# A streaming decode block: GpSimd's half-sums taken out, pairs of heads evicted inside PSUM, one weight block split differently

## The chip, the cores and the metric

The kernel runs on one core of a Trainium2 chip. The metric is device microseconds from one execution, the median of three runs. Lower is better.

## The reference

One token goes through an adaptive-LayerNorm block with cached attention and a squared-ReLU feed-forward part. All data are float32, D = 640, 32 heads of 192, 8192 cached keys and values per head, feed-forward width 1536.

```python
mod = (silu(c) @ w_mod).reshape(1, 6, 1, 640)      # sa, ca, ga, sb, cb, gb
h = layernorm(x) * (1 + ca) + sa
q = (h @ wq) split into 32 heads of 192
p = softmax(q . k_cache * 192**-0.5)               # 32 x 8192
x = x + ga * ((p . v_cache) joined @ wo)
h = layernorm(x) * (1 + cb) + sb
x = x + gb * (relu(h @ w1 + b1)**2 @ w2 + b2)
```

The two caches are 201 MB each; every byte of them is read once.

## The kernel before, in words

The caches and the weights `wq` and `wo` are laid out on the host as 53 chunks, each one slice of at most 84 x 192 = 16128 floats in each of the 128 partitions. `plan()` (L55) writes down what each chunk holds: some key positions (`nk`, 64 positions per partition make a head), some units of values (`nv`, eight units make a head) and now and then a piece of `wq` or `wo`. Most chunks hold 44 key positions and 5 value units.

All loads go through SyncE's one queue, in program order, into three slots of SBUF that are used in turn. `load(n + 3)` (L240) may start when everything that reads chunk n is done, so the queue is at most three chunks ahead. The first slot of all holds `wm0`, the first two modulation blocks with the first piece of `wq` (L122), and behind it `wm0x`: part of the columns of the last of its five row blocks, 128 rows, which the table `XP` deals over some of 64 partitions in up to seven steps and which six small loads bring (L125). A small load has 8, 3 or 1 of these partitions.

For the keys of a chunk VectorE does nearly everything. `multiply` (L273) multiplies every key with the query in place. Then, for the last 7/16 of the chunk's positions, GpSimd adds the upper 96 of the 192 products to the lower 96 (L399, "folds" them), while VectorE sums the other 9/16 (`scores`, L281). VectorE then sums the folded positions over 96 elements. Scores stand in a ring `sc`. When a head's 64 positions are complete, `softmax` takes the maximum over partitions with a TensorE transpose and ScalarE writes the exponentials `p`. For an odd head, ScalarE spreads the two sums of a pair (`wide`), TensorE turns them over the partitions (L310), and `inverse` sums the result (L288) and takes its reciprocal.

For the values, TensorE multiplies `p` with each unit (L322) into one PSUM bank per head. The bank holds eight products side by side of which a mask picks one. `evict` (L334, L336) multiplies by the mask into SBUF and sums over the eight, for each head apart; after an odd head TensorE transposes the pair (L340) and VectorE sums over the copies (`turn`, L344). `attend` (L352 to L356) then multiplies with `wo` into `att_a`.

After the last chunk come the other modulation blocks (`mod(2, 3)`, `gate`), the second LayerNorm, `w1` (L447), the squared ReLU, and `w2` (L464), whose four pieces are the last loads of the queue.

Of the kernel before, what the change touches and what calls it, by code (L numbers as in the profile page):

```python
# [93 lines left out]
def block_kernel(ctx: ExitStack, tc: tile.TileContext, kv, wm0, wm0x, wm1, w1, w2, out):  # L94
# [89 lines left out]
    def mod(first, n, w, wx=None, between=lambda: None):  # L184

        ps = psum.tile([P, 512], F32, tag="q", name=f"ps_mod{first}", bufs=2)
        for b in range(KB):
            if b == 3:
                between()
            wb = w[:, b * n * D:(b + 1) * n * D]  # L190
            if wx is None or b < KB - 1:
                wb = wb.rearrange("p (m n) -> p m n", m=n)
                parts = [(g, slice(0, n * DG), wb[:, :, DG * g:DG * (g + 1)]) for g in range(G)]
            else:
                wb = wb[:, :n * 3 * DG].rearrange("p (m n) -> p m n", m=n)
                parts = [(g, slice(0, n * DG), wb[:, :, DG * g:DG * (g + 1)]) for g in range(2)] + [(2, slice(0, DG), wb[:, 0, 2 * DG:])]
            for g, at, wg in parts:
                nc.tensor.matmul(ps[32 * g:32 * (g + 1), at], e[:, b:b + 1].to_broadcast([P, 32]), wg,  # L198
                                 start=(b == 0), stop=(b == KB - 1 and (wx is None or g < 2)))
# [86 lines left out]
    def inverse(i):  # L286
        r = work.tile([P, 1], F32, tag="r", name=f"r{i}")
        nc.vector.tensor_reduce(r, sum_t.pop(i), axis=AX.X, op=ALU.add)  # L288
        nc.vector.reciprocal(r, r)
        ri_t[i] = r  # L290

    def softmax(h):
# [34 lines left out]
    def evict(h):  # L327

        n = 32 * NV
        if h % 2 == 0:  # L330
            os_t["part"] = work.tile([P, 2, ED], F32, tag="os", name=f"os{h // 2}")
        os_ = os_t["part"]
        om = work.tile([P, ED, E], F32, tag="om", name=f"om{h}", bufs=1)
        nc.vector.tensor_mul(om[:n], ps_t.pop(h)[:n].rearrange("p (d e) -> p d e", e=E),  # L334
                             mask[:n, None, :].to_broadcast([n, ED, E]))
        nc.vector.tensor_reduce(os_[:n, h % 2], om[:n], axis=AX.X, op=ALU.add)  # L336
        if h % 2:
            i = h // 2
            os_t[i] = psum.tile([P, 512], F32, tag="sm", name=f"ps_oT{i}", bufs=2)
            nc.tensor.transpose(os_t[i][:, :n], os_[:n].rearrange("p a d -> p (a d)"), ident[:n, :n])  # L340

    def turn(i):
        oT = work.tile([P, NV], F32, tag="oT", name=f"oT{i}")
        nc.vector.tensor_reduce(oT, os_t[i][:, :96].rearrange("p (j r) -> p j r", j=NV), axis=AX.X, op=ALU.add)  # L344
        os_t[i] = oT
# [177 lines left out]
```

## Time and profile before

| | |
|---|---|
| median of three runs | 1051.96 us (1051.89 to 1052.2) |
| the profiled execution, its own time | 1051.94 us |
| its span, from the first to the last instruction | 1050.0 us |
| VectorE busy | 826.1 us (79%) |
| TensorE busy | 488.7 us (47%) |
| GpSimd busy | 190.4 us (18%) |
| DMA | 452.14 MB, mean 431 GB/s |

The execution's own time is 1.94 us longer than its span. The profile names an instruction by its line in the kernel, its engine, and output <- input by the program's names. DVE is VectorE, PE TensorE (PEld its weight loads), ACT ScalarE, POOL GpSimd and SP SyncE. "Idle" is the time an engine stood still ahead of an instruction, and behind the arrow stands what ended it.

### The profile page before, as it was taken

What the parts mean: (1) busy time and instruction counts of PE and PEld (TensorE: products, weight loads), DVE (VectorE), ACT (ScalarE), POOL (GpSimd) and SP (SyncE); (2) the same over time, 40 slices, a digit from 0 to 9 for tenths busy, and PEclk for the clock granted to TensorE, in tenths of its full rate; (3) what the DMA queues carried; (4) which work ended last, traced back from release to release, by engine and by line L of the source; (5) the groups of instructions that cost most, each with busy time, mean ns of one, the idle gap of its engine ahead of it and who ended that gap; (6) DMA issues with size and microseconds to landing.
All of it is one profiled execution on the core that took longest, in us unless ns stands there. A gap on an engine that the chain in (4) does not pass through costs nothing.

```text
span 1050.0 us, 5180 instructions
## 1 busy us (share of the span) xinstructions
PE 488.7 (47%) x2130; PEld 133.8 (13%) x2130; DVE 826.1 (79%) x405; ACT 44.9 (4%) x122; POOL 190.4 (18%) x61
## 2 busy tenths in 40 slices
PE   3253334455352363446354356345445346435287
PEld 1010001111010010101011011001011011001023
DVE  1799878876959969888697895999887977988812
ACT  0100000000000000000000000000000000000001
POOL 1113121121212211212121121122211211311200
PEclk9676576777685686668776576686777767768689
DMA  9999999999999999999999999999999999999998
GB/s 408 430 433 432 434 435 433 446 439 433 431 432 433 428 433 433 433 442 434 432 434 433 433 434 437 435 433 435 436 430 433 433 435 433 435 433 426 431 429 345
DMA packets 9144, 452.14 MB, mean 431 GB/s; under 512 B 1033, under 2 KB 1037, under 8 KB 1421
## 3 DMA queue, kind: packets, MB, share of 16 engines
q1 hardware_dynamic: 9118, 451.83, 99.5%
q8 instruction: 16, 0.26, 0.1%
q14 instruction: 6, 0.05, 0.0%
q10 hardware_dynamic: 4, 0.00, 0.0%
HBM read 451.82 MB, written 0.00 MB: 430 GB/s over the span
## 4 chain that ended last, share of the span: by engine, by line
DMA 53%; DVE 33%; PE 12%; ACT 1%; issue 0%; SPq 0%; DVEq 0%; ACTq 0%
DMA chunk<-in_kv 50%; DVE chunk L273 17%; DVE sc L281 13%; PE ps_o L322 6%; PE ps_q L254 2%; PE att_a L354 2%; DMA w_t<-in_w 2%; DMA wm_t<-in_wm 1%; DVE os L336 1%; DVE om L334 1%; PE ps_mx L297 1%; PE att_a L356 1%; ACT p L305 0%; PE ps_mod L198 0%; PE ps_mod L204 0%
## 5 line engine op out<-in xcount | busy, mean ns | idle before, releaser
L273 DVE TENSOR_TENSOR chunk<-chunk,qb 128x8064 f32<-128x8064 f32 (+19 forms) x81 | 419.6, 5211 | 127.3 <-DMA chunk<-in_kv 122.1
L281 DVE TENSOR_REDUCE sc<-chunk 128x25 f32<-128x4800 f32 (+21 forms) x109 | 333.8, 3096 | 0.4
L399 POOL TENSOR_TENSOR chunk<-chunk 128x1824 f32<-128x1824 f32 (+9 forms) x51 | 187.3, 3673 | 801.0 <-DVE chunk L273 568.6
L322 PE MATMUL ps_o<-chunk,p 128*32 128x512 f32 x1536 | 288.6, 719 | 70.1 <-DMA chunk<-in_kv 60.6
L297 PE MATMUL ps_mx<-ident,mp 128*128 128x128 f32 x32 | 14.6, 457 | 347.6 <-DVE mp L295 347.5
L322 PEld LDWEIGHTS ps_o<-chunk,p 128*32 128x32 f32 x1536 | 66.2, 129 | 268.1 <-issue 183.2
L354 PE MATMUL att_a<-chunk,oW 128*32 128x512 f32 x96 | 66.5, 850 | 45.0 <-ACT oW L352 45.0
L254 PE MATMUL ps_q<-chunk,ln_h 128*128 128x512 f32 x110 | 64.5, 746 | 25.2 <-DMA chunk<-in_kv 25.2
L297 PEld LDWEIGHTS ps_mx<-ident,mp 128*128 128x128 f32 x32 | 5.7, 177 | 376.3 <-DVE mp L295 308.2
L305 ACT ACTIVATE p<-sc,nm 128x256 f32<-128x256 f32 x32 | 16.2, 507 | 651.0 <-DVE nm L299 651.0
L254 PEld LDWEIGHTS ps_q<-chunk,ln_h 128*128 128x128 f32 x110 | 25.9, 246 | 61.6 <-issue 33.1
L334 DVE TENSOR_TENSOR om<-ps_o,mask 96x512 f32<-96x512 f32 x32 | 21.6, 675 | 8.9 <-PE ps_o L322 8.9
L299 DVE TENSOR_REDUCE nm<-ps_mx 128x1 f32<-128x128 f32 x32 | 9.3, 292 | 19.6 <-PE ps_mx L297 19.6
L354 PEld LDWEIGHTS att_a<-chunk,oW 128*32 128x32 f32 x96 | 12.4, 145 | 82.4 <-ACT oW L352 47.6
L336 DVE TENSOR_REDUCE os<-om 96x64 f32<-96x512 f32 x32 | 21.8, 682 | 1.1
L344 DVE TENSOR_REDUCE oT<-ps_oT 128x3 f32<-128x96 f32 x16 | 4.0, 248 | 18.4 <-PE ps_oT L340 18.4
L310 PE MATMUL ps_sum<-ident,wide 128*128 128x128 f32 x16 | 7.5, 467 | 22.4 <-ACT wide L308 22.4
L340 PE MATMUL ps_oT<-ident,os 96*128 96x96 f32 x16 | 4.9, 306 | 26.9 <-DVE os L336 26.9
L198 PE MATMUL ps_mod<-wm_t,silu 128*32 128x480 f32 (+2 forms) x78 | 9.1, 606 | 14.4 <-DVE silu L180 14.4
L356 PE MATMUL att_a<-chunk,oW 128*96 128x384 f32 x32 | 14.5, 536 | 0.0
L352 ACT ACTIVATE oW<-oT,r 128x96 f32<-128x96 f32 x16 | 5.9, 372 | 173.3 <-DVE oT L344 173.3
L255 ACT ACTIVATE qb<-ps_q 128x512 f32<-128x512 f32 x12 | 7.2, 597 | 130.6 <-PE ps_q L254 130.6
(79 smaller groups left out, 99.8 us busy)
## 6 DMA issues: line engine op xcount, KB each, us to landing
chunk<-in_kv SPq DMA_DIRECT2D x38, 8064.0 KB, 35.3
chunk<-in_kv SPq DMA_DIRECT2D x11, 8000.0 KB, 36.6
chunk<-in_kv SPq DMA_DIRECT2D x2, 7872.0 KB
chunk<-in_kv SPq DMA_DIRECT2D x1, 6144.0 KB, 22.8
wm_t<-in_wm SPq DMA_DIRECT2D x1, 4480.0 KB
wm_t<-in_wm SPq DMA_DIRECT2D x1, 4257.0 KB, 12.5
chunk<-in_kv SPq DMA_DIRECT2D x1, 3264.0 KB
chunk<-in_kv SPq DMA_DIRECT2D x1, 3072.0 KB
```

The source lines that it names most:

```text
L254: nc.tensor.matmul(ps, h1[:, b:b + 1].to_broadcast([P, P]), w[:, b], start=(b == 0), stop=(b == KB - 1))
L273: nc.vector.tensor_mul(pr, pr, q[:, None, :].to_broadcast([P, b - a, DH]))
L281: nc.vector.tensor_reduce(sc[:, a % SRING:a % SRING + b - a], src[:, a - first:b - first], axis=AX.X, op=ALU.add)
L297: nc.tensor.transpose(ps[:, :P], mp.to_broadcast([P, P]), ident)
L299: nc.vector.tensor_reduce(nm, ps[:, :P], axis=AX.X, op=ALU.max, negate=True)
L305: nc.scalar.activation(p, s[:, :, None].to_broadcast([P, NPOS, 32 // E]), AF.Exp, bias=nm, accum_out=sp[:, h % 2:h % 2 + 1])
L322: nc.tensor.matmul(ps_t[h][32 * g:32 * (g + 1)], p[:, E * j:E * (j + 1)].rearrange("p e r -> p (e r)"), t[:, g], start=(j == 0), stop=last)
L334: nc.vector.tensor_mul(om[:n], ps_t.pop(h)[:n].rearrange("p (d e) -> p d e", e=E), mask[:n, None, :].to_broadcast([n, ED, E]))
L336: nc.vector.tensor_reduce(os_[:n, h % 2], om[:n], axis=AX.X, op=ALU.add)
L354: nc.tensor.matmul(att_a[96:, :512], oW[:, j], w[:, j, :512], start=(first and j == 0), stop=(last and j == NV - 1))
L356: nc.tensor.matmul(att_a[:96, :NV * (D - 512)], oW.rearrange("p j r -> p (j r)"), w[:, :, 512:], start=first, stop=last)
L399: nc.gpsimd.tensor_add(half, half, kt[:, m:, DH // 2:])
```

## The change

1. GpSimd no longer folds. `scores` gets the whole chunk, so VectorE sums all positions over 192 elements in one instruction. The ring `sc` is twice as long, so that it wraps half as often.
2. Pairs of heads share one PSUM tile of two banks (two such tiles in place of three single banks). `evict` multiplies by the mask in place in PSUM and sums, once for a pair (for the last pair, once for each head).
3. The sum over the copies (`turn`) goes to TensorE: the matmul at the end of `evict` has `part` (ones for each group of 32 rows) where the identity was, and its three columns are the result. The sum in `inverse` goes there as well, by a matmul with ones.
4. PSUM tag `q` has one bank in place of two. `ps_f` moves to the tag of the pairs.
5. The last block of `wm0` (640 columns for each of its two modulations) is split so that the small loads carry 4 x 160 columns of each row in place of 3 x 160, and `XP` deals them in other portions. `mod(0, 2)` reads them with 28 passes of 320 columns where it had 14 of 160 and 14 of 320.
6. Two copies at the start (`spread`) go from VectorE to ScalarE.

```diff
-POOL = 7
-SRING = 4 * NPOS
+SRING = 8 * NPOS
-XP = ((32, 8, 5), (0, 3, SX), (1, 3, SX), (2, 3, SX), (3, 3, 6), (33, 1, SX))
-WX = 3 * DG
+XP = ((32, 8, SX), (33, 8, 4), (0, 3, SX), (1, 3, 3), (2, 1, SX), (3, 1, 3))
+WX = 4 * DG
...
         if wx is not None:
...
-                for g, at, wg in ((2, slice(DG, 2 * DG), wx[:, s, :DG]), (3, slice(0, 2 * DG), wx[:, s, DG:])):
-                    nc.tensor.matmul(ps[32 * g:32 * (g + 1), at], e[:64, KB + s:KB + s + 1].to_broadcast([64, 32]), wg,
-                                     start=False, stop=(s == SX - 1))
+                for g in range(2, G):
+                    nc.tensor.matmul(ps[32 * g:32 * (g + 1), :n * DG], e[:64, KB + s:KB + s + 1].to_broadcast([64, 32]),
+                                     wx[:, s, g - 2], start=False, stop=(s == SX - 1))
...
     def gate(m, w, steps):
 
-        ps = psum.tile([P, 512], F32, tag="q", name=f"ps_mod{m}", bufs=2)
+        ps = psum.tile([P, 512], F32, tag="q", name=f"ps_mod{m}", bufs=1)
...
     def inverse(i):
         r = work.tile([P, 1], F32, tag="r", name=f"r{i}")
-        nc.vector.tensor_reduce(r, sum_t.pop(i), axis=AX.X, op=ALU.add)
-        nc.vector.reciprocal(r, r)
+        nc.vector.reciprocal(r, sum_t.pop(i))
...
-            nc.tensor.transpose(ps[:, :P], wide.rearrange("p a d -> p (a d)"), ident)
-            sum_t[h // 2] = ps[:, :P]
+            nc.tensor.matmul(ps[:, :1], wide.rearrange("p a d -> p (a d)"), ones[:, :1], start=True, stop=True)
+            sum_t[h // 2] = ps[:, :1]
...
-        if j == 0:
-            ps_t[h] = psum.tile([P, 512], F32, tag="o", name=f"ps_o{h}", bufs=3)
+        if j == 0 and h % 2 == 0:
+            ps_t[h // 2] = psum.tile([P, 2, 512], F32, tag="o", name=f"ps_o{h // 2}", bufs=2)
...
+    def evict(first, last):
+
+        n, i = 32 * NV, first // 2
+        a, b = first % 2, last % 2 + 1
+        po = ps_t[i][:n, a:b].rearrange("p a (d e) -> p a d e", e=E)
+        nc.vector.tensor_mul(po, po, mask[:n, None, None, :].to_broadcast([n, b - a, ED, E]))
+        if a == 0:
+            os_t[i] = work.tile([P, 2, ED], F32, tag="os", name=f"os{i}")
+        nc.vector.tensor_reduce(os_t[i][:n, a:b], po, axis=AX.X, op=ALU.add)
+        if b == 2:
+            nc.tensor.matmul(ps_t[i][:, 0, :NV], os_t.pop(i)[:n].rearrange("p a d -> p (a d)"), part[:n, :NV],
+                             start=True, stop=True)
...
         if nk:
             multiply(kt, kp, nk)
-            m = nk - POOL * nk // 16
-            half = kt[:, m:, :DH // 2]
-            nc.gpsimd.tensor_add(half, half, kt[:, m:, DH // 2:])
...
-        for h in evicted:
-            evict(h)
+        for heads in evicted:
+            evict(*heads)
         if nk:
-            scores(kt[:, :m], kp)
-        for h in evicted:
-            if h % 2:
-                turn(h // 2)
-        if nk:
-            scores(half, kp + m)
+            scores(kt, kp)
```

How the instructions stand on VectorE for the third and fourth chunk, before (44 key positions each; `ps_o` is a head's PSUM bank, `sc` the ring of scores):

```order
L273 TENSOR_TENSOR chunk_178<-chunk_178,qb 128x6528
L273 TENSOR_TENSOR chunk_178<-chunk_178,qb 128x1920
L281 TENSOR_REDUCE sc<-chunk_178 128x25
L281 TENSOR_REDUCE sc<-chunk_178 128x19
L295 TENSOR_REDUCE mp_238<-sc 128x1
L299 TENSOR_REDUCE nm_242<-ps_mx_240 128x1
L273 TENSOR_TENSOR chunk_193<-chunk_193,qb 128x8448
L288 TENSOR_REDUCE r_276<-ps_sum_248 128x1
L289 RECIPROCAL r_276<-r_276 128x1
L334 TENSOR_TENSOR om_280<-ps_o_202,mask 96x512
L336 TENSOR_REDUCE os_279<-om_280 96x64
L281 TENSOR_REDUCE sc<-chunk_193 128x25
```

The same place in the changed kernel:

```order
L280 TENSOR_TENSOR chunk_179<-chunk_179,qb 128x6528
L280 TENSOR_TENSOR chunk_179<-chunk_179,qb 128x1920
L288 TENSOR_REDUCE sc<-chunk_179 128x44
L301 TENSOR_REDUCE mp_233<-sc 128x1
L305 TENSOR_REDUCE nm_237<-ps_mx_235 128x1
L280 TENSOR_TENSOR chunk_192<-chunk_192,qb 128x8448
L295 RECIPROCAL r_269<-ps_sum_243 128x1
L288 TENSOR_REDUCE sc<-chunk_192 128x44
```

The two sums of 25 and 19 positions have become one of 44, and the first head's eviction is no longer in the fourth chunk: it waits for the second head.

VectorE from the last chunk with keys to the end of attention, before (`om`, `os` and `oT` are the steps of an eviction):

```order
L273 TENSOR_TENSOR chunk_1865<-chunk_1865,qb 128x8064
L334 TENSOR_TENSOR om_1955<-ps_o_1840,mask 96x512
L336 TENSOR_REDUCE os_1954<-om_1955 96x64
L281 TENSOR_REDUCE sc<-chunk_1865 128x24
L281 TENSOR_REDUCE sc<-chunk_1865 128x18
L295 TENSOR_REDUCE mp_1960<-sc 128x1
L299 TENSOR_REDUCE nm_1964<-ps_mx_1962 128x1
L288 TENSOR_REDUCE r_2004<-ps_sum_1970 128x1
L289 RECIPROCAL r_2004<-r_2004 128x1
L334 TENSOR_TENSOR om_2007<-ps_o_1910,mask 96x512
L336 TENSOR_REDUCE os_1954<-om_2007 96x64
L344 TENSOR_REDUCE oT_2012<-ps_oT_2010 128x3
```

And in the changed kernel, up to the last eviction:

```order
L280 TENSOR_TENSOR chunk_1643<-chunk_1643,qb 128x8064
L288 TENSOR_REDUCE sc<-chunk_1643 128x42
L301 TENSOR_REDUCE mp_1723<-sc 128x1
L305 TENSOR_REDUCE nm_1727<-ps_mx_1725 128x1
L295 RECIPROCAL r_1766<-ps_sum_1733 128x1
L338 TENSOR_TENSOR ps_o_1624<-ps_o_1624,mask 96x1024
L341 TENSOR_REDUCE os_1769<-ps_o_1624 96x128
L338 TENSOR_TENSOR ps_o_1738<-ps_o_1738,mask 96x512
L341 TENSOR_REDUCE os_1803<-ps_o_1738 96x64
L338 TENSOR_TENSOR ps_o_1738<-ps_o_1738,mask 96x512
L341 TENSOR_REDUCE os_1803<-ps_o_1738 96x64
```

No eviction stands between the last multiply and the last sum any more, a pair's eviction follows the last softmax, and the `oT` sums are gone.

TensorE behind the last attention product, before (with the semaphores that each instruction waits for; `ps_mod_2066` is `mod(2, 3)`, `ps_mod_2102` is `gate`):

```order
L198 MATMUL ps_mod_2066<-wm_t,silu 32x480 [waits DMAHW6_49]
L198 MATMUL ps_mod_2066<-wm_t,silu 32x480 x7
L215 MATMUL ps_mod_2102<-wm_t,silu 64x320 x4
L150 MATMUL ps_ln_tm<-ln_s,ones 128x1 [waits DVE_49,PE_49]
L215 MATMUL ps_mod_2102<-wm_t,silu 64x320 x2
L150 MATMUL ps_ln_tv<-ln_ss,ones 128x1 [waits DVE_49,PE_49]
```

The same in the changed kernel:

```order
L205 MATMUL ps_mod_1819<-wm_t,silu 32x480 [waits DMAHW6_49]
L205 MATMUL ps_mod_1819<-wm_t,silu 32x480 x7
L222 MATMUL ps_mod_1855<-wm_t,silu 64x320 [waits DVE_49]
L222 MATMUL ps_mod_1855<-wm_t,silu 64x320 x3
L155 MATMUL ps_ln_tm<-ln_s,ones 128x1 [waits DVE_49]
L222 MATMUL ps_mod_1855<-wm_t,silu 64x320 x2
L155 MATMUL ps_ln_tv<-ln_ss,ones 128x1 [waits DVE_49]
```

The order is the same, but `gate` now waits for VectorE: it has to write the one bank that VectorE is still copying `mod(2, 3)` from.

## Rows read from the trace of the kernel before

**Rows 1.** The page: busy time of each engine, then the load queue's share.

```profile
PE 488.7 (47%) x2130; PEld 133.8 (13%) x2130; DVE 826.1 (79%) x405; ACT 44.9 (4%) x122; POOL 190.4 (18%) x61
...
q1 hardware_dynamic: 9118, 451.83, 99.5%
```

**Rows 2.** Stretches of the span: length, busy times, PE clock, DMA share, GB/s.

```profile
0.00:1.70 1.70, 0.00 (x0) 0.00 (x0) 0.35 (x2) 0.97 (x1) 1.10 (x9) 1.00 0.00 0
...
20.00:1020.00 1000.00, 459.78 (x1863) 122.14 (x1859) 816.36 (x378) 39.52 (x110) 187.31 (x51) 0.71 1.00 434
...
1043.00:1046.10 3.10, 2.25 (x63) 1.58 (x56) 0.00 (x0) 0.00 (x0) 0.00 (x0) 1.00 0.72 294
1046.10:1050.00 3.90, 0.85 (x20) 0.21 (x12) 0.65 (x2) 0.00 (x0) 0.00 (x0) 0.85 0.00 1
```

**Rows 3.** The page's groups by line: count, busy us, mean ns, idle before.

```profile
L273 DVE TENSOR_TENSOR chunk<-chunk,qb 128x8064 f32<-128x8064 f32 (+19 forms) x81 | 419.6, 5211 | 127.3 <-DMA chunk<-in_kv 122.1
L281 DVE TENSOR_REDUCE sc<-chunk 128x25 f32<-128x4800 f32 (+21 forms) x109 | 333.8, 3096 | 0.4
L399 POOL TENSOR_TENSOR chunk<-chunk 128x1824 f32<-128x1824 f32 (+9 forms) x51 | 187.3, 3673 | 801.0 <-DVE chunk L273 568.6
...
L344 DVE TENSOR_REDUCE oT<-ps_oT 128x3 f32<-128x96 f32 x16 | 4.0, 248 | 18.4 <-PE ps_oT L340 18.4
```

**Rows 4.** VectorE's groups by line and form.

```profile
L281 DVE TENSOR_REDUCE sc<-chunk 128x25 f32<-128x4800 f32 x23 | 118.3, 5144 | 0.3
...
L281 DVE TENSOR_REDUCE sc<-chunk 128x19 f32<-128x1824 f32 x23 | 46.9, 2040 | 0.0
...
L336 DVE TENSOR_REDUCE os<-om 96x64 f32<-96x512 f32 x32 | 21.8, 682 | 1.1
L334 DVE TENSOR_TENSOR om<-ps_o,mask 96x512 f32<-96x512 f32 x32 | 21.6, 675 | 8.9 <-PE ps_o L322 8.9
...
L288 DVE TENSOR_REDUCE r<-ps_sum 128x1 f32<-128x128 f32 x16 | 4.6, 285 | 1.5 <-PE ps_sum L310 1.5
```

**Rows 5.** The page's DMA issues: count, KB each, median us from issue to landing.

```profile
chunk<-in_kv SPq DMA_DIRECT2D x38, 8064.0 KB, 35.3
chunk<-in_kv SPq DMA_DIRECT2D x11, 8000.0 KB, 36.6
...
chunk<-in_kv SPq DMA_DIRECT2D x1, 6144.0 KB, 22.8
...
wm_t<-in_wm SPq DMA_DIRECT2D x1, 4257.0 KB, 12.5
```

**Rows 6.** The timeline's start: start us, us, what, idle before.

```profile
18.98 3.96 PE L204 MATMUL ps_mod<-wm_t,silu 64*32 64x160 f32 x28
...
34.89 12.96 DVE L273 TENSOR_TENSOR chunk<-chunk,qb 128x12288 f32<-128x12288 f32 x1 [5.11 <-ACT qb L255]
47.88 10.21 DVE L281 TENSOR_REDUCE sc<-chunk 128x36 f32<-128x6912 f32 x2
...
106.26 9.03 DVE L273 TENSOR_TENSOR chunk<-chunk,qb 128x1920 f32<-128x1920 f32 x2 [1.33 <-DMA chunk<-in_kv]
```

**Rows 7.** The timeline of SyncE's queue: issues of loads 3 and 7.

```profile
58.12 0.33 SPq L240 DMA_DIRECT2D chunk<-in_kv  x1
...
129.34 0.33 SPq L240 DMA_DIRECT2D chunk<-in_kv  x1
```

**Rows 8.** The timeline's end, from the last keys to the last weights.

```profile
979.39 8.56 DVE L273 TENSOR_TENSOR chunk<-chunk,qb 128x8064 f32<-128x8064 f32 x1 [1.36 <-DMA chunk<-in_kv]
...
989.18 6.80 DVE L281 TENSOR_REDUCE sc<-chunk 128x24 f32<-128x4608 f32 x2
...
1030.82 0.66 DVE L206 COPY mods<-ps_mod 128x480 f32<-128x480 f32 x1 [3.77 <-PE ps_mod L198]
...
1042.02 1.84 PE L464 MATMUL ps_y<-w_t,fT 128*32 128x160 f32 x48 [1.00 <-DMA w_t<-in_w]
...
1045.72 1.25 PE L464 MATMUL ps_y<-w_t,fT 128*32 128x160 f32 x24 [0.49 <-DMA w_t<-in_w]
```

More of the change, by code (lines that the diff above doesn't have):

```diff
@@ L114, in block_kernel @@
     nc.vector.tensor_reduce(sel, ident.rearrange("p (g c) -> p c g", g=G)[:, 0], axis=AX.X, op=ALU.add)
+    part = const.tile([P, G], F32, name="part")
+    nc.vector.tensor_reduce(part, ident.rearrange("p (g c) -> p g c", g=G), axis=AX.X, op=ALU.add)
     eps_t = const.tile([P, 1], F32, name="eps_t")
@@ L184, in mod @@
     def mod(first, n, w, wx=None, between=lambda: None):
-        ps = psum.tile([P, 512], F32, tag="q", name=f"ps_mod{first}", bufs=2)
+        ps = psum.tile([P, 512], F32, tag="q", name=f"ps_mod{first}", bufs=1)
         for b in range(KB):
@@ L192, in mod @@
                 wb = wb.rearrange("p (m n) -> p m n", m=n)
-                parts = [(g, slice(0, n * DG), wb[:, :, DG * g:DG * (g + 1)]) for g in range(G)]
+                parts = [(g, wb[:, :, DG * g:DG * (g + 1)]) for g in range(G)]
             else:
[L195 to L199, printed above, removed]
+                wb = wb[:, :n * 2 * DG].rearrange("p (m n) -> p m n", m=n)
+                parts = [(g, wb[:, :, DG * g:DG * (g + 1)]) for g in range(2)]
+            for g, wg in parts:
+                nc.tensor.matmul(ps[32 * g:32 * (g + 1), :n * DG], e[:, b:b + 1].to_broadcast([P, 32]), wg,
+                                 start=(b == 0), stop=(b == KB - 1))
         if wx is not None:
-            wx = wx.rearrange("p (s n) -> p s n", s=SX)
+            wx = wx.rearrange("p (s g n) -> p s g n", s=SX, g=2)
             for s in range(SX):
-                for g, at, wg in ((2, slice(DG, 2 * DG), wx[:, s, :DG]), (3, slice(0, 2 * DG), wx[:, s, DG:])):
-                    nc.tensor.matmul(ps[32 * g:32 * (g + 1), at], e[:64, KB + s:KB + s + 1].to_broadcast([64, 32]), wg,
-                                     start=False, stop=(s == SX - 1))
+                for g in range(2, G):
+                    nc.tensor.matmul(ps[32 * g:32 * (g + 1), :n * DG], e[:64, KB + s:KB + s + 1].to_broadcast([64, 32]),
+                                     wx[:, s, g - 2], start=False, stop=(s == SX - 1))
         nc.vector.tensor_copy(mods[:, first:first + n], ps[:, :n * DG].rearrange("p (m n) -> p m n", m=n))
     def gate(m, w, steps):
-        ps = psum.tile([P, 512], F32, tag="q", name=f"ps_mod{m}", bufs=2)
+        ps = psum.tile([P, 512], F32, tag="q", name=f"ps_mod{m}", bufs=1)
         b = 0
@@ L321, in values @@
         for g in range(NV):
-            nc.tensor.matmul(ps_t[h][32 * g:32 * (g + 1)], p[:, E * j:E * (j + 1)].rearrange("p e r -> p (e r)"),
+            nc.tensor.matmul(ps_t[h // 2][32 * g:32 * (g + 1), h % 2], p[:, E * j:E * (j + 1)].rearrange("p e r -> p (e r)"),
                              t[:, g], start=(j == 0), stop=last)
     os_t = {}
[L327 to L336, printed above, removed]
-        if h % 2:
[L338 to L345, printed above, removed]
+    def evict(first, last):
[9 more added lines that the diff above has]
+                             start=True, stop=True)
     def attend(i, w):
-        oT = os_t.pop(i)
+        oT = ps_t.pop(i)[:, 0, :NV]
         w = w.rearrange("p (j n) -> p j n", j=NV)
@@ L419, in block_kernel @@
         for v in range(vp, vp + nv):
[L420 to L421 removed]
+            h = v // (NPOS // E)
+            if v % (NPOS // E) == NPOS // E - 1 and (h % 2 or h == H - 2):
+                to_evict.append((h if h >= H - 2 else h - 1, h))
         if wo_t is not None and n + 1 < len(PLAN):
@@ L429, in block_kernel @@
     w2_t = w2_t[:, :FB * D].rearrange("p (b n) -> p b n", b=FB)
-    for h in to_evict:
-        evict(h)
-    turn(NPAIR - 1)
+    for heads in to_evict:
+        evict(*heads)
     attend(*wo_t)
@@ L454, in block_kernel @@
     nc.vector.scalar_tensor_tensor(f, f, 0.0, f, op0=ALU.max, op1=ALU.mult)
-    fT = columns(f, FG, "fT", work, tag="om", bufs=1)
+    fT = columns(f, FG, "fT", work, bufs=1)
     gb2 = const.tile([P, DG], F32, name="gb2")
@@ L508 @@
         "kv": np.concatenate(kv),
-        "wm0": np.concatenate([m0[:, :(KB - 1) * 2 * D], last[:, 0, :3 * DG], last[:, 1, :2 * DG],
+        "wm0": np.concatenate([m0[:, :(KB - 1) * 2 * D], last[:, 0, :2 * DG], last[:, 1, :2 * DG],
                                wq[0], column(A_x, KB), cc, cx, column(B_b1, FB), column(B_b2, KB)], axis=1),
```

33 lines of the change are left out of this document (17 added, 16 removed).

## The prediction

> **What bounds the kernel now.** I read the engines' busy times first, then the load queue, then the stretches, and last the places where the queue could run dry. VectorE is the busiest engine with 826.1 of 1050.0 us, but the loads' packets fill 99.5% of what sixteen DMA engines could do in the span [rows 1], that is 1044.7 us. The stretches say where the rest lies [rows 2]: nothing moves in the first 1.70 us and in the last 3.90 us, in the thousand microseconds between 20 and 1020 the DMA share is 1.00 at 434 GB/s, and only from 1043.0 to 1046.1 is it 0.72, because some of the sixteen finish before others. So the time is 1.7 us of start, a stream that never stops, and a tail. An engine matters only where it makes the stream stop or lengthens the tail.
>
> VectorE does wait: of its idle time ahead of the multiplies, 122.1 us end with the arrival of a chunk [rows 3]. It has spare time on average, and the question is where it has none.
>
> The queue's lead over it is seen in the loads [rows 5]. A usual chunk of 8064 KB streams in 8064 x 1024 / 434e3 = 19.0 us, and it lands 35.3 us after its issue. Some 16 us are thus spent in line behind other loads. A load may be issued that much later before the stream notices.
>
> **The change, part by part.** *The sums on VectorE.* A sum over 4800 elements takes 5144 ns and one over 1824 takes 2040 ns [rows 4]: 3104/2976 = 1.043 ns per element and 138 ns for each instruction. A usual chunk of 44 positions (8448 elements) took 5.14 + 2.04 = 7.18 us and will take 8.95, so +1.77 us. Over all keys 2048 x 192 = 393216 elements make 410 us, and some 55 instructions 7.6 us more: 417.7 against 333.8 [rows 3], +83.9 us. What goes away on GpSimd, 51 folds with 187.3 us [rows 3], stood on nobody's way.
>
> *Evictions.* Today a head costs 675 + 682 ns [rows 4], 43.4 us in all. A pair in one instruction adds 512 elements at 1.043 ns: 1.21 us each for product and sum. Fifteen pairs and two single heads: 15 x 2.43 + 2 x 1.36 = 39.1 us, -4.3. No row shows VectorE writing PSUM. It reads PSUM at its usual rate (the `om` product, 675 ns for 512), so I take that price; the lower bound is no saving at all over that, the upper one twice the price (the product would pay once for reading and once for writing), +18 us for products, or +37 if the sums pay too. The `oT` sums (4.0 us and 18.4 us of waiting [rows 3]) and the `r` sums (4.6 us [rows 4]) leave VectorE; their matmuls are tiny on a TensorE that is 47% busy [rows 1].
>
> Together VectorE gets 83.9 - 4.3 - 4.0 - 4.6 = +71 us and loses 18.4 us of waits. That fits into the 122.1 us that it waits for chunks. In chunks: 44 positions cost 2 x 8.95 us plus about 1 us of softmax, and the stream needs 19.0 us. The densest five chunks by `plan()` hold 228 positions in 95 us of stream; at 0.4 us each they take 91 us and some 7 us of softmax and evictions, a lag of about 3 us against 16 us of lead. In the middle this costs nothing.
>
> *The start.* Here VectorE has no idle time to give. Load 3 needs chunk 0 done. It is issued at 58.12 [rows 7], and the stream reaches it after 4257 + 240 + 6144 + 8000 + 8064 KB [rows 5] (the 240 are 128 x 480 floats of small loads), 27.35 MB at 434 GB/s, so at 1.7 + 63.0 = 64.7 us. The sums of chunk 0 took 10.21 us [rows 6] and will take 12.95. The query may also come at another time: the 28 passes of `wx` took 3.96 us [rows 6]; if they cost by columns, 8960 for 6720, that is +1.3 us, and if the shorter pass ran beside the longer one, nothing. I take +0.3. Load 3 is then issued at 61.2, 3.5 us ahead. The first load of the program needed at most 1.7 us from the program's start to its first bytes [rows 2], so no stop.
>
> The lag grows until VectorE first waits for a chunk, which today is for 1.33 us at 106.26 [rows 6]. Chunk 0: 3.0, chunk 1 (5760 elements): 1.2, chunks 2, 3 and 4: 5.3, less one eviction (1.36) and the `r` sum (0.28), less that wait: 6.5 us. Load 7, which follows chunk 4, is issued at 129.34 [rows 7] and is due after four more chunks, at 140.7 us. It had 11.4 us and keeps 4.9. Stop again none, with some 3 us in hand. Behind it the lag shrinks.
>
> *The load itself.* The bytes are the same. Each row of `wm0` gets 640 bytes shorter, 8 rows for an engine, 5120 bytes at 434/16 = 27.1 GB/s: -0.19 us on each of sixteen. The small loads grow by 81920 bytes. Spread evenly that is +0.19; put on few engines it is more. If a load of k rows goes to k engines, always the same first ones, the first engine got 39 pieces of 1920 bytes and gets 31 of 2560: 2.76 to 2.93 us, +0.17, net nothing; the last five of the eight go from 5 pieces to 11, 0.35 to 1.04 us, net +0.50; the other eight gain the full 0.19. The Trainium skill says so ("DMA: Bandwidth & Descriptors", section on why a DMA increments its semaphore by 16): a load uses the largest number of engines up to 16 that divides its rows, the lowest-numbered ones. No view shown here names the engine of a packet. What counts are the engines that end last. As most end late [rows 2], I take -0.1 us, with bounds -0.2 and +0.5.
>
> *The tail.* The last chunk with keys starts after a wait of 1.36 us for its arrival [rows 8]; VectorE will come 1.8 us later from the chunk before, so it starts 0.4 us later. Its sums took 6.80 us and take 8.55, but an eviction of 1.36 us no longer stands between: +0.8 us. The `oT` sum behind the last eviction goes, -0.25. `gate` waits for the copy of `mod(2, 3)`, at most its 0.66 us [rows 8], of which part was waited elsewhere; +0.2. In sum the chain is 0.75 us later, at most 1.2. Its cover: the products with `w2` wait 1.00 us for their first piece and 0.49 us for a later one [rows 8]. So nothing reaches the end; beyond 1.5 us it would, one for one.
>
> Sum, against the execution's own 1051.94 us (span 1050.0 and 1.94 around it, 0.02 under the median): 0 for VectorE, 0 for the start, -0.1 for the load, 0 for the tail: 1051.84, say **1051.8 us**.
>
> One more rule speaks of this change. The Trainium skill ("SBUF — State Buffer", section on its two sides) has GpSimd and VectorE exclude each other at a shared port when a GpSimd operation that reads SBUF meets a VectorE operation with two SBUF inputs. By it VectorE's multiplies would gain from a silent GpSimd. The trace shows no loss to win back: 12288 products in 12.96 us [rows 6] are 1.04 ns each besides the fixed part, VectorE's full rate, and a fold always waits for its chunk's multiply [rows 3].
>
> **The rivals.** *The stream stops at the start (slower).* Load 3 or load 7 comes too late: VectorE would have to be over 1.8 us later than I work out at load 3 or over 3.2 at load 7, from a late query or slower wide sums. From there each microsecond costs one. A query 4 us late gives 1054.0; sums 15% slower add 1.9 us in chunk 0, 0.9 in chunk 1 and 1.3 in each of the next three, 6.7 us by load 7, which then stops the stream for 3.5 us: 1055.3. For it: these are the smallest margins. Against it: all its parts are durations that the trace has.
>
> *The tail slips (a little slower).* Products and sums in PSUM at twice the price make the last eviction 1.4 us longer; the chain is then 2.2 to 2.6 us later, and 0.7 to 1.1 us come through: 1052.8. It decides from 1.5 us on.
>
> *The uneven deal helps.* If the sixteen ended together, the 0.28 x 3.1 us left idle [rows 2] would go: at best 1051.94 - 0.87 = 1051.1. *Or it hurts:* if one of the five engines with +0.50 is among the last, 1052.4.
>
> That the change takes load off the time as it takes it off GpSimd can't be: GpSimd ends no wait on the stream's path.
>
> **How the numbers follow.** A measurement of this kernel can tell about 0.2% (2.1 us) from no change. Forecast, 1051.4 to 1052.2: 0.60. A better deal, 1050.9 to 1051.4: 0.10. A worse deal or a slipped tail, 1052.2 to 1054.0: 0.20. Stops, above 1054.0: 0.08. Something unseen that takes over 2.1 us away: 0.02. Faster by over 0.2% is thus 0.02, slower 0.08, the same 0.90. The range that leaves out less than 0.2 goes from 1050.9 to 1053.2.
>
> **What would show it.** VectorE busy near 897 us, its waits for chunks down from 122 to about 70 us, wide sums of 8.95 us for 44 positions, GpSimd almost silent, evictions of a pair of 1.2 us each for product and sum, load 3 issued near 61 us and load 7 near 136, a DMA share of 1.00 from 20 to 1020 us, and `w2` products that still wait for their pieces. The prediction is wrong if the DMA share dips anywhere before 1043 us, if the last products start after their weights have landed, or if the stream's last microseconds change by more than half a microsecond.

## The result, and the profile after

The changed kernel takes **1055.31 us** (median of 7 runs, 1055.08 to 1055.94), the kernel before 1051.97 us beside it (7 runs, 1051.89 to 1052.26). The ratio is 1.0032, 95% interval 1.002 to 1.0044: 3.3 us slower, where 1051.8 and no change were forecast. The profiled execution took 1055.94 us, 0.63 above the median, with a span of 1054.2.

The page of the changed kernel, engines and load queue, answers to [rows 1]:

```profile
PE 491.8 (47%) x2160; PEld 142.6 (14%) x2160; DVE 901.0 (85%) x287; ACT 45.2 (4%) x124; POOL 3.6 (0%) x10
...
q1 hardware_dynamic: 9124, 451.83, 99.3%
```

VectorE is busy for 75 us more and GpSimd for next to nothing. The queue, which was full to 99.5% of 1050.0 us, is full to 99.3% of 1054.2: 1046.8 us of packets in place of 1044.7, for the same 451.83 MB. The bytes have become dearer.

The groups by line and form, answering to [rows 3, 4]:

```profile
L288 DVE TENSOR_REDUCE sc<-chunk 128x44 f32<-128x8448 f32 x23 | 205.9, 8953 | 0.5
...
L341 DVE TENSOR_REDUCE os<-ps_o 96x128 f32<-96x1024 f32 x15 | 18.3, 1220 | 0.5
L338 DVE TENSOR_TENSOR ps_o<-ps_o,mask 96x1024 f32<-96x1024 f32 x15 | 18.3, 1218 | 0.0
```

and of the page's groups the multiplies:

```profile
L280 DVE TENSOR_TENSOR chunk<-chunk,qb 128x8064 f32<-128x8064 f32 (+19 forms) x81 | 419.5, 5210 | 66.5 <-DMA chunk<-in_kv 59.8
```

VectorE does what the prediction says at the prices that it says, and still waits 59.8 us for chunks. SyncE's queue, with the issues of loads 3 and 7 ([rows 7]):

```profile
61.24 0.33 SPq L247 DMA_DIRECT2D chunk<-in_kv  x1
...
136.51 0.33 SPq L247 DMA_DIRECT2D chunk<-in_kv  x1
```

Both are where they were forecast. The stretches, as in [rows 2], with those at the end shifted:

```profile
20.00:1020.00 1000.00, 459.79 (x1874) 130.03 (x1873) 888.23 (x256) 39.03 (x110) 0.00 (x0) 0.71 1.00 433
...
1043.00:1046.10 3.10, 3.10 (x34) 1.14 (x27) 0.46 (x1) 0.27 (x1) 0.00 (x0) 1.00 0.94 388
1046.10:1049.10 3.00, 2.83 (x48) 1.79 (x50) 1.76 (x5) 0.00 (x0) 0.00 (x0) 1.00 0.57 227
1049.10:1054.10 5.00, 2.02 (x60) 1.70 (x52) 0.65 (x2) 0.00 (x0) 0.00 (x0) 1.00 0.02 5
```

The stream never stops: a DMA share of 1.00 over the middle thousand microseconds. But it runs at 433 GB/s where it ran at 434, and it ends about 3 us later. One GB/s in 434 over 1044 us is 2.4 us. The end of the timeline:

```profile
963.74 4.56 DVE L280 TENSOR_TENSOR chunk<-chunk,qb 128x4224 f32<-128x4224 f32 x1 [2.50 <-DMA chunk<-in_kv]
...
1023.83 0.70 DVE L338 TENSOR_TENSOR ps_o<-ps_o,mask 96x512 f32<-96x512 f32 x1 [18.60 <-PE ps_o L328]
1024.56 0.69 DVE L341 TENSOR_REDUCE os<-ps_o 96x64 f32<-96x512 f32 x1
1025.28 0.70 DVE L338 TENSOR_TENSOR ps_o<-ps_o,mask 96x512 f32<-96x512 f32 x1
1026.01 0.69 DVE L341 TENSOR_REDUCE os<-ps_o 96x64 f32<-96x512 f32 x1
...
1047.66 3.47 PE L455 MATMUL ps_y<-w_t,fT 128*32 128x160 f32 x96 [0.17 <-DVE gb L449]
```

Two things are to be seen. Head 30's eviction starts at 1023.83, after head 31's products (it waits 18.60 us for L328), so that the two single evictions stand in a row; before, head 30's ran 10 us ahead of head 31's:

```profile
1008.21 0.68 DVE L334 TENSOR_TENSOR om<-ps_o,mask 96x512 f32<-96x512 f32 x1
...
1018.53 0.69 DVE L334 TENSOR_TENSOR om<-ps_o,mask 96x512 f32<-96x512 f32 x1 [8.93 <-PE ps_o L322]
```

And the 96 products with `w2` run in one piece, waiting for VectorE and for no data. In [rows 8] they waited twice for their weights. In this execution the tail's chain, not the stream, sets the end.

### The profile page after: what moved, and what is told of

The parts are those of the page before. It is cut to its first block, busy times and chain, and to the rows that moved or that the text cites. A ratio compares the mean times of both kernels' runs of the same rounds, so it can differ in the third digit from the quotient of the medians.

```text
span 1054.2 us, 4943 instructions
## 1 busy us (share of the span) xinstructions
PE 491.8 (47%) x2160; PEld 142.6 (14%) x2160; DVE 901.0 (85%) x287; ACT 45.2 (4%) x124; POOL 3.6 (0%) x10
## 3 DMA queue, kind: packets, MB, share of 16 engines
q1 hardware_dynamic: 9124, 451.83, 99.3%
## 4 chain that ended last, share of the span: by engine, by line
DVE 51%; DMA 36%; PE 10%; ACT 1%; issue 1%; DVEq 0%; SPq 0%; ACTq 0%
DMA chunk<-in_kv 34%; DVE chunk L280 24%; DVE sc L288 24%; PE ps_o L328 5%; DMA wm_t<-in_wm 1%; PE att_a L353 1%; PE ps_mx L303 1%; PE ps_mod L205 1%; DVE os L341 1%; DVE ps_o L338 1%; PE ps_q L261 1%; DVE nm L305 1%; ACT p L311 1%; PE ps_sum L316 0%; DVE mp L301 0%
## 5 line engine op out<-in xcount | busy, mean ns | idle before, releaser
L280 DVE TENSOR_TENSOR chunk<-chunk,qb 128x8064 f32<-128x8064 f32 (+19 forms) x81 | 419.5, 5210 | 66.5 <-DMA chunk<-in_kv 59.8
L288 DVE TENSOR_REDUCE sc<-chunk 128x44 f32<-128x8448 f32 (+12 forms) x54 | 417.4, 7733 | 0.8
L328 PE MATMUL ps_o<-chunk,p 128*32 128x512 f32 x1536 | 300.1, 744 | 68.8 <-DMA chunk<-in_kv 59.6
L328 PEld LDWEIGHTS ps_o<-chunk,p 128*32 128x32 f32 x1536 | 67.9, 132 | 271.8 <-issue 190.1
L353 PE MATMUL att_a<-chunk,oW 128*32 128x512 f32 x96 | 54.3, 711 | 6.0 <-ACT oW L351 6.0
L338 DVE TENSOR_TENSOR ps_o<-ps_o,mask 96x1024 f32<-96x1024 f32 (+1 forms) x17 | 19.7, 1157 | 18.6 <-PE ps_o L328 18.6
L343 PE MATMUL ps_o<-part,os 96*128 96x3 f32 x32 | 7.1, 291 | 34.5 <-DVE os L341 34.5
L341 DVE TENSOR_REDUCE os<-ps_o 96x128 f32<-96x1024 f32 (+1 forms) x17 | 19.7, 1158 | 0.6
L316 PE MATMUL ps_sum<-ones,wide 128*128 128x1 f32 x32 | 9.4, 362 | 21.7 <-ACT wide L314 21.7
L205 PE MATMUL ps_mod<-wm_t,silu 128*32 128x480 f32 (+1 forms) x76 | 9.2, 620 | 14.6 <-DVE silu L187 14.6
L343 PEld LDWEIGHTS ps_o<-part,os 96*128 96x128 f32 x32 | 5.9, 226 | 48.2 <-DVE os L341 44.7
L316 PEld LDWEIGHTS ps_sum<-ones,wide 128*128 128x128 f32 x32 | 8.0, 311 | 26.3 <-ACT wide L314 26.3
```

The source lines that it names most:

```text
L205: nc.tensor.matmul(ps[32 * g:32 * (g + 1), :n * DG], e[:, b:b + 1].to_broadcast([P, 32]), wg, start=(b == 0), stop=(b == KB - 1))
L280: nc.vector.tensor_mul(pr, pr, q[:, None, :].to_broadcast([P, b - a, DH]))
L288: nc.vector.tensor_reduce(sc[:, a % SRING:a % SRING + b - a], src[:, a - first:b - first], axis=AX.X, op=ALU.add)
L316: nc.tensor.matmul(ps[:, :1], wide.rearrange("p a d -> p (a d)"), ones[:, :1], start=True, stop=True)
L328: nc.tensor.matmul(ps_t[h // 2][32 * g:32 * (g + 1), h % 2], p[:, E * j:E * (j + 1)].rearrange("p e r -> p (e r)"), t[:, g], start=(j == 0 ...
L338: nc.vector.tensor_mul(po, po, mask[:n, None, None, :].to_broadcast([n, b - a, ED, E]))
```

## What the stream's price could come from

The trace holds each packet of the loads, one for the row of each partition. Those of a usual chunk, 64512 bytes for one partition, took 2380 ns in the median before and 2384 ns after (mean 2381.6 and 2386.7, 4864 packets each). It is not a stop at a few places but a little on every packet, once it has set in: of these packets that start after 200 us all take longer than 2380 ns, and before the change 0.4% of them did. Those that start between 38 and 76 us, into the same slots, take 2380 ns in the median in both kernels. The theories:

- **Address.** The three slots that the stream is loaded into lie behind the constants. `part` and the ring `sc`, which is twice as long, take 1056 bytes more per partition (32 and 1024), so the slots begin at byte 26400 in place of 25344 (both are read from the built programs). 25344 is 99 x 256; 26400 leaves a remainder of 32. A slot is 252 x 256 bytes long, so all three have the same remainder.
- **Work.** VectorE's 75 us more, or GpSimd's absence, change what SBUF has to serve while the loads write.

A third, **deal**, is that the new portions of `XP` make one of the sixteen engines late; and a fourth, **tail**, that the chain behind the last chunk is too long for its cover.

## The experiments

Each is timed against the kernel before on the same chip.

| run | kernel | slots at | median us | ratio, 95% interval |
|---|---|---|---|---|
| e1 | before, constant of 1056 bytes | 26400 | 1054.62 | 1.0026, 1.0015 to 1.0038 |
| e2 | changed, constant of 224 bytes | 26624 | 1053.10 | 1.0010, 1.0001 to 1.0018 |
| e3 | before, GpSimd's fold out | 25344 | 1052.69 | 1.0009, 1.0000 to 1.0018 |
| e4 | before, new deal | 25344 | 1052.40 | 1.0003, 0.9995 to 1.0012 |
| e5 | e2, early evictions | 26624 | 1052.50 | 1.0003, 0.9994 to 1.0012 |
| e6 | e2, deal of before | 26624 | 1052.87 | 1.0006, 0.9998 to 1.0015 |
| e7 | e2, early evictions, deal of before | 26624 | 1051.95 | 0.9999, 0.9990 to 1.0007 |
| e8 | before, constant of 64 bytes | 25408 | 1054.35 | 1.0023, 1.0013 to 1.0032 |
| e9 | before, constant of 128 bytes | 25472 | 1054.10 | 1.0019, 1.0011 to 1.0028 |
| e10 | before, constant of 256 bytes | 25600 | 1051.99 | 0.9999, 0.9990 to 1.0007 |
| e11 | changed, early evictions, deal of before | 26400 | 1054.63 | 1.0024, 1.0014 to 1.0033 |
| e12 | changed, early evictions | 26400 | 1055.38 | 1.0029, 1.0018 to 1.0041 |

The medians of before are 1052.04 (e1 to e4), 1052.07 (e5 to e8), 1052.01 (e9 to e11) and 1052.13 (e12), each group on a chip of its own. The intervals of e1, e8, e9, e11 and e12 lie clear of 1; those of e3 to e7 and e10 hold it or touch it, and e2's nearly does. Differences of less than 1 us between these rows are differences of medians, and the text says where the runs behind them overlap.

### Address against work (e1, e2, e3)

e1 and e2 add an unused constant ahead of the slots, 264 floats to the kernel before, 56 to the changed one:

```diff
+    pad = const.tile([P, 264], F32, name="pad")
+    nc.gpsimd.memset(pad[:, :1], 0.0)
     eps_t = const.tile([P, 1], F32, name="eps_t")
```

e1. 

> The kernel before with one unused constant of 1056 bytes per partition (and a one-column memset at the start), so that the three slots that the stream is loaded into begin at byte 26400 of a partition, where the changed kernel has them, in place of 25344. Nothing else changes: GpSimd folds, VectorE's work, the deal and the tail are those of before. Theory 'address': the stream's loads are slower because of where the slots begin; then a chunk takes some 0.05 us longer (about 19.06 in place of 19.01 us), the last data land 2 to 3 us later, and the time is 1053.5 to 1055.0 us, a good half of the change's loss. Rival 'work': the stream is slowed by what the engines do to SBUF (VectorE summing 71 us more, GpSimd gone), or by the new deal; then this kernel takes 1051.7 to 1052.4 us, as before.

e2. 

> The changed kernel with an unused constant of 224 bytes, so that its slots begin at byte 26624, a multiple of 256 again (25344 was one, 26400 is not). Theory 'address': the chunks come every 19.01 us again and the last data land 2 to 3 us earlier than in the changed kernel, near 1046.1 to 1047; the end then hangs on the tail's chain, which has its own added 1 to 2 us: 1052.0 to 1053.6 us. Rival 'work': 1055.0 to 1056.0 us, as the changed kernel.

e3 leaves the fold out of the kernel before:

```diff
-            m = nk - POOL * nk // 16
-            half = kt[:, m:, :DH // 2]
-            nc.gpsimd.tensor_add(half, half, kt[:, m:, DH // 2:])
...
-            scores(kt[:, :m], kp)
+            scores(kt, kp)
...
-        if nk:
-            scores(half, kp + m)
```

> The kernel before with GpSimd's fold left out: VectorE sums all positions of a chunk in one instruction after the evictions, and the oT sum stays where it was. Slots begin at byte 25344 as before; evictions, deal and tail are those of before, but for the last chunks' sums, which are longer. Theory 'address': VectorE's 71 us more cost nothing in the stream, and the time is 1051.6 to 1052.6 us. Rival 'work': the stream slows as in the changed kernel, 1053.5 to 1055 us.

Measured: e1 loses 2.58 us with nothing changed but where the slots, and the constants between the pad and them, lie, and e2 wins 2.2 of the 3.3 us back with the whole change in place. The arrivals show it along the stream. VectorE waits for chunk 4 and for chunk 50 in both kernels; in e1:

```profile
106.20 2.16 DVE L275 TENSOR_TENSOR chunk<-chunk,qb 128x1920 f32<-128x1920 f32 x1 [1.44 <-DMA chunk<-in_kv]
...
981.83 8.56 DVE L275 TENSOR_TENSOR chunk<-chunk,qb 128x8064 f32<-128x8064 f32 x1 [1.37 <-DMA chunk<-in_kv]
```

875.63 us between them, where [rows 6, 8] have 979.39 - 106.26 = 873.13: 2.50 us more over 46 chunks, 0.05 us each. e1's packets take 2384 ns in the median, those of e2 2380. In e2 chunk 49 is there 2.4 us earlier than in the changed kernel:

```profile
961.34 4.56 DVE L282 TENSOR_TENSOR chunk<-chunk,qb 128x4224 f32<-128x4224 f32 x1 [2.35 <-DMA chunk<-in_kv]
```

The rival *work* has nothing left of this: in e3 VectorE is busy for 909.8 us, longer than in the changed kernel, and the packets take 2380 ns in the median. (Their mean, 2385.3, is that of a stop: 25 packets of 2.5 to 3.9 us start between 139 and 148 us, and without those over 2450 ns it is 2380.2, as before.) But e3 is 0.65 us slower, 0.1 above the range of *address*, for another reason. Its issue of load 7, then its stretches there, then those of the changed kernel:

```profile
140.08 0.33 SPq L240 DMA_DIRECT2D chunk<-in_kv  x1
```

```profile
120.00:140.00 20.00, 6.82 (x26) 1.57 (x26) 19.33 (x8) 0.60 (x2) 0.00 (x0) 0.52 0.97 420
140.00:146.00 6.00, 6.00 (x25) 2.29 (x25) 5.61 (x1) 0.60 (x1) 0.00 (x0) 1.00 0.92 323
```

```profile
120.00:140.00 20.00, 9.23 (x34) 3.00 (x35) 19.33 (x8) 0.60 (x2) 0.00 (x0) 0.64 1.00 430
140.00:146.00 6.00, 5.57 (x31) 1.55 (x30) 6.00 (x3) 0.94 (x2) 0.00 (x0) 1.00 0.93 399
```

With single evictions and the `oT` and `r` sums still on VectorE, load 7 comes 3.6 us later than in the changed kernel, and behind it the queue moves 323 GB/s for six microseconds. The landings show it more plainly: sixteen signals end a load, and the first of them comes as early as before up to load 6, is 1.43 us later for load 7 and stays 1.4 to 1.5 us later to the end. This is the prediction's first rival, reached by half of the change; pairs and TensorE's sums keep the whole change clear of it. How much of the 0.65 us it is stays open: e3's profiled execution, at 1054.88 us, was the longest of its eleven runs.

### Which addresses (e8, e9, e10)

The same edit on the kernel before, with 16, 32 and 64 floats.

e8. 

> The kernel before with an unused constant of 64 bytes: the slots begin at byte 25408, a multiple of 64 but not of 256 (remainder 64). Theory 'address, whole lines of 256 bytes': the packets of the chunks take as long as at byte 26400 and the time is about 1054.6 us. Rival 'address, 64 bytes do': packets as at byte 25344 and 1051.9 to 1052.3 us. In between (1052.8 to 1054.0): the loss goes by the remainder.

e9. 

> The kernel before with an unused constant of 128 bytes: the slots begin at byte 25472, remainder 128 from a multiple of 256. If only a multiple of 256 will do, the time is 1053.5 to 1054.7 us, as at remainder 32 (1054.62) and 64 (1054.35); if a multiple of 128 does, 1051.9 to 1052.3 us.

e10. 

> The control: the kernel before with an unused constant of 256 bytes, which takes the same memset and moves every later constant as the others do, but leaves the slots at a multiple of 256 (25600). Theory 'address': 1051.8 to 1052.3 us and packets as before. Rival: it is the added constant itself, or the constants that it moves, that cost; then 1054 us or more.

Remainders of 32 (e1), 64 and 128 cost 2.58, 2.28 and 2.09 us; remainder 0 costs nothing, at 25600 as at 25344 and 26624. So a multiple of 64 or of 128 will not do. The intervals of the three overlap; the mean packets, 2386.5, 2385.0 and 2385.0 ns, set 32 apart from the other two. e10 is the control: the constant itself, its memset and the shift of what lies behind it are free. Its arrivals:

```profile
106.14 2.16 DVE L275 TENSOR_TENSOR chunk<-chunk,qb 128x1920 f32<-128x1920 f32 x1 [0.94 <-DMA chunk<-in_kv]
...
979.54 8.56 DVE L275 TENSOR_TENSOR chunk<-chunk,qb 128x8064 f32<-128x8064 f32 x1 [1.31 <-DMA chunk<-in_kv]
```

873.40 us, and packets of 2380 ns; in e9 it is 981.17 - 106.38 = 874.79 us:

```profile
106.38 2.16 DVE L275 TENSOR_TENSOR chunk<-chunk,qb 128x1920 f32<-128x1920 f32 x1 [1.43 <-DMA chunk<-in_kv]
...
981.17 8.56 DVE L275 TENSOR_TENSOR chunk<-chunk,qb 128x8064 f32<-128x8064 f32 x1 [1.45 <-DMA chunk<-in_kv]
```

The Trainium skill ("DMA: Bandwidth & Descriptors", section on how a descriptor splits into AXI transactions) says that a descriptor which doesn't start at a multiple of 256 bytes fetches the bytes ahead of its start too, and pays for them in beats of 32 bytes. It says so of reading; what was moved here is the address written to. By its beats, an estimate, a row of 64512 bytes would take 1 beat more in 2016 at remainder 32, 2 at 64 and 4 at 128, some 0.5 to 2.1 us over the stream. The multiple agrees with the runs, the order doesn't: remainder 32 measures dearest.

Two things these runs leave open. The pad moves the constants and work tiles behind it by as many bytes as the slots; that the slots' start is what counts, and not that of something the engines read, is argued and not shown. For it speaks that the dearer packets write slots alone, and that VectorE's prices stay (a product of 8064 takes 8555 ns in e1 as before). And the address is not all: the first loads pay nothing at byte 26400, in e1 as in the changed kernel. What sets the price off some 100 us into the stream no run tells.

### Deal and tail (e4, e5, e6, e7)

e4 puts the new `XP`, `WX` and products of `mod(0, 2)` into the kernel before, as the diff of the change shows them; e6 and e7 take them out of e2. e5 and e7 write the evictions of the two chunks without keys ahead of their products (head 30's, and the pair's before it, so that a gain is that of both):

```diff
+        if not nk:
+            for heads in to_evict:
+                evict(*heads)
+            to_evict = []
         for v in range(vp, vp + nv):
             if v not in late:
```

e4. 

> The kernel before with the new deal of the 640 columns alone (more rows, wider parts, the products that go with it); slots begin at byte 25344 as before. Theories 'address' and 'work' both give 1051.5 to 1052.3 us: a few KB more or less on one engine, up to 0.5 us either way at the end of the stream. Rival 'deal': the uneven deal makes one engine late by 1 us or more over the whole stream, and the time is 1053 us or more; the lead of the fastest engine over the slowest then grows from 3.0 towards 3.6 us.

e5. 

> The changed kernel with its slots at byte 26624, as in the second run, and in the last chunk the eviction of head 30 written ahead of head 31's products, so that it need not wait for them. Theory 'tail': with the slots right again the end is set by the chain through the last evictions; 1.4 us of single evictions leave it, the last products then wait for the last data (1046.4 us in the second run) again, and the time falls by 0.4 to 0.6 us from 1053.1 to about 1052.6 us. Rival 'stream alone': the end follows the last data already, and nothing changes (1053.0 to 1053.2 us).

e6. 

> The changed kernel with its slots at byte 26624 and the deal of the 640 columns of before. Theory 'tail': the last data land some 0.4 us earlier and the chunks of the end too, but the chain through the last evictions keeps its 1.4 us, so the time falls by 0.2 to 0.5 us, to 1052.6 to 1052.9 us. Rival 'stream alone': the time follows the last data, which land where they did before, so 1052.0 to 1052.2 us.

e7. 

> Both edits of the two runs beside it: slots at byte 26624, head 30 evicted ahead of head 31's products, deal of before. Theory 'tail': what is left of the change is VectorE's whole sums, pair evictions and TensorE's two sums, which then cost nothing: 1051.8 to 1052.3 us, the time of before. Rival: something else in the change still costs (the single mod bank that makes the gate's products wait 0.78 us, the longer sums of the last chunks), and the time stays at 1052.5 us or more.

e5, e6 and e7 fall where *tail* puts them. e4 lies 0.1 us above the range of *address* and well below that of *deal* as it was stated: the deal is no matter of 1 us, but by the medians it costs 0.36 us (the interval holds 1; all eleven runs of e4 lie above 23 of the 29 of before). The last chunk with keys comes later than in [rows 8] (979.39, after 1.36 us of waiting), since the sixteen signals of its landing spread over 4.06 us, before over 3.03:

```profile
980.40 8.56 DVE L273 TENSOR_TENSOR chunk<-chunk,qb 128x8064 f32<-128x8064 f32 x1 [2.13 <-DMA chunk<-in_kv]
```

That lateness is not there from the first loads on. Up to the chunk that lands at 600 us the last signal comes 0.2 to 0.3 us earlier in e4's trace than before; then it falls behind mainly in two steps, by 0.39 us up to the next chunk and by 0.77 us between 961 and 979 us. Into each of the two falls a load of the program's own code (610.3 and 966.9 us), as it does before (610.1 and 965.9), where the steps were smaller. Which of the sixteen engines a row or a piece of code falls on, no row shows.

The deal costs 0.23 us from e6 to e2, whose runs overlap, and 0.55 from e7 to e5, whose runs don't. The early evictions bring 0.60 us from e2 to e5 and 0.92 from e6 to e7, both without overlap. In e2 the products with `w2` ran in one piece, as in the changed kernel; in e7 they wait for their weights again, as in [rows 8]:

```profile
1044.29 3.47 PE L457 MATMUL ps_y<-w_t,fT 128*32 128x160 f32 x96 [0.17 <-DVE gb L451]
```

```profile
1042.16 1.84 PE L461 MATMUL ps_y<-w_t,fT 128*32 128x160 f32 x48 [0.80 <-DMA w_t<-in_w]
1044.36 1.02 PE L461 MATMUL ps_y<-w_t,fT 128*32 128x160 f32 x24 [0.37 <-DMA w_t<-in_w]
1045.91 1.25 PE L461 MATMUL ps_y<-w_t,fT 128*32 128x160 f32 x24 [0.53 <-DMA w_t<-in_w]
```

The scatter says the same: e2 and e6, where the chain ends last, spread over 1.2 and 1.1 us, e5 and e7 over 0.3 and 0.4. At 1051.95 us e7 stands where the kernel before stands (1052.07): VectorE's whole sums, the pairs in PSUM and TensorE's sums are free, as forecast, and win nothing, since the stream still sets the time. No version here beats the kernel before.

### Does it add up (e11, e12)

e11. 

> The changed kernel with the deal of before and head 30 evicted early, but with its slots left at byte 26400. If the address's price does not depend on the tail, it stands 2.3 to 2.7 us above the same kernel at byte 26624 (1051.95 us), at 1054.2 to 1054.7 us, and the address is most of the change's loss of 3.3 us. Rival: the three causes overlap, and with the tail mended the later data matter less; below 1053.8 us.

e12. 

> The changed kernel with the evictions of the two chunks without keys written ahead of their products, and nothing else: slots at byte 26400, the new deal. It closes the sum. If the three causes add up, it stands 0.3 to 0.6 us above the same kernel with the deal of before (1054.63 us), at 1054.9 to 1055.2 us, and 0.1 to 0.4 us below the changed kernel (1055.31 us). Rival: with the data 2.6 us later the tail's chain is covered and the early eviction is worth nothing, 1055.3 us or more.

e11 differs from e7 in the pad alone: 2.68 us. e12 over e11 is the deal at byte 26400: 0.75 us. But e12 is not below the changed kernel (1055.38 against 1055.31): the causes don't add, and the rival of e12 holds. Its products with `w2` wait for data:

```profile
1045.47 1.84 PE L459 MATMUL ps_y<-w_t,fT 128*32 128x160 f32 x48 [1.31 <-DMA w_t<-in_w]
1047.70 1.02 PE L459 MATMUL ps_y<-w_t,fT 128*32 128x160 f32 x24 [0.39 <-DMA w_t<-in_w]
1049.29 1.27 PE L459 MATMUL ps_y<-w_t,fT 128*32 128x160 f32 x24 [0.56 <-DMA w_t<-in_w]
```

So the loss of 3.3 us is the address (2.7) and the deal (some 0.7), and the tail's chain is about level with the late stream: mending it lowers no median there. It may shorten the longest executions, of which the profiled one is one (e12's seven runs end at 1055.51 us, the changed kernel's at 1055.94), and it counts once the address is mended.

## Why the prediction was wrong, by its own steps

**"The load itself", the step that failed.** It says that the bytes are the same and takes -0.1 us. The bytes were the same and their price was not: the constants that the change adds move the slots off a multiple of 256 bytes, which costs 2.1 to 2.7 us in e1, e8, e9 and e11 over e7. No rival named it. What the step should have asked is at what price the same bytes come. The trace of before can't show it; the list of what lies ahead of the slots could have raised the question. The deal in the same step was bounded by -0.2 and +0.5 with -0.1 taken; it measures +0.36 by itself and 0.2 to 0.75 in company. The sign taken was wrong. That the rival "hurts" gave 1052.4 and e4 took 1052.40 is luck: it has five engines late from the first loads on, and in e4's trace the last signals are not late before 600 us. Whether the dealt bytes make an engine late at all, or how the loads of code fall beside them, is not settled.

**"The tail", wrong in size.** The own lateness of VectorE up to the last sums was forecast at 0.8 us and is 1.0: the sums end 3.94 us later (999.92 for the 989.18 + 6.80 = 995.98 of [rows 8]), 2.95 of it the later chunk 49.

```profile
991.37 8.55 DVE L288 TENSOR_REDUCE sc<-chunk 128x42 f32<-128x8064 f32 x1
```

What the sum left out is head 30's eviction, which the shared tile holds back behind head 31's products: a row of two, 1.45 us. And the products in between take 10.73 us where they took 9.10. These two stretches, of the kernel before and of the changed one (the clock is the number ahead of the last two), show the granted clock at 0.86 and at 0.73:

```profile
998.60:1007.70 9.10, 9.10 (x56) 2.22 (x55) 1.72 (x4) 0.00 (x0) 0.00 (x0) 0.86 1.01 437
```

```profile
1002.50:1013.20 10.70, 10.70 (x55) 2.56 (x55) 2.51 (x3) 0.00 (x0) 0.00 (x0) 0.73 1.03 437
```

Both begin at the lower of the two levels, 1.2 GHz, and end at the higher, 2.4 GHz. In the changed kernel the weight loads of three products follow one another after 0.85 us at the lower (1003.43, 1004.28) and after 0.43 us at the higher (1008.85, 1009.28). TensorE, which had stood still for some 10 us ahead of both stretches, gets the higher level later here; why was not tried. The cover of 1.5 us was also too small a reading of [rows 8]: the chain of e2 is 3.1 us later than before (the transpose into `fT` ends at 1044.03 in place of 1040.93), and its `y` comes 0.77 us later (1047.81 for 1047.04), so some 2.3 us were covered.

**Right.** VectorE +71 us (75 measured) on its free time, sums of 8.95 us (8.953), pairs of 1.21 us (1.218 and 1.220, so PSUM written in place costs nothing extra), load 3 at 61.2 (61.24), load 7 at 136.0 (136.51), waits for chunks down from 122 (to 59.8, not 70), multiplies that gain nothing from a silent GpSimd (419.5 us in all, 419.6 before), and a stream that doesn't stop. The rival of slower products and sums in PSUM falls with the pairs' price; the rival of the stop at load 7 was not met, though e3 shows how near it lies: load 7 only 3.6 us later. By the prediction's margin, 3.2 us behind 136.0, a load issued at 140.08 stops the stream for 0.9 us; the landings of e3 show 1.43. And of what would prove the prediction wrong, the third did, a stream that ends over half a microsecond later, as did the second in the profiled execution. With address, deal and evictions put right, e7 takes 1051.95 us where 1051.8 was forecast.

## What to carry to other kernels

Where a stream of loads sets the time, count what a change adds to the memory ahead of the load buffers, and try their start at a multiple of 256 bytes; a pad of 224 bytes was worth 2.2 us here. When two results are put into one tile, ask which readers now wait for both. A tail's cover is how much later its last link may become ready before the end moves; the waits that its last rows show can be less than that (1.00 and 0.49 us in [rows 8], where 2.3 us were covered).

## What the runs showed of the hardware

- The time of a load's packets went with the start of the slots: 2380 ns for 64512 bytes at 25344, 25600 and 26624, 2384 at 26400, 2382 at 25408, 2384 at 25472 (means 2381.6, 2381.5, 2381.6, 2386.5 in e1, 2385.0, 2385.0). It did so only after the first 100 us or so: between 38 and 76 us the median was 2380 in e1, e8, e9 and the changed kernel too.
- The program's own code is loaded beside the stream in pieces of 16384 bytes, 16 or 17 in an execution. They took 933 to 938 ns in the median where the slots began at a multiple of 256 and 1065 to 1069 ns where they did not, though they are not written into the slots. They go with late engines: from one chunk's landing to the next, the spread of its sixteen signals grows by more than 0.25 us 23 times in the fourteen traces, and 21 times such a piece is loaded in between, as it is for 213 of all 708 chunks. The changed kernel's largest step is 1.34 us, with a piece at 607 us.
